# Dense products beside column-tiled runs turned into column tiles, in a fused attention and SwiGLU block on Trainium2

## The chip, the core and the metric

The kernel runs on one core of one Trainium2 chip. A core has TensorE (PE in the profile, PEld for its weight loads), VectorE (DVE), ScalarE (ACT), GpSimd (POOL) and SyncE (SP, which here issues every DMA). The metric is the device time of one execution in microseconds, as the median of several runs; lower is better. Each instruction belongs to one engine's queue and runs there in the order in which it was written; engines wait for one another through semaphores.

## What is computed

A pre-LayerNorm transformer block on 2048 tokens of width 1024, in bf16. Its attention is split into 4 segments of 512 tokens, with 32 heads of 32 elements. Within a segment it is ordinary softmax attention; in addition a memory M (32x32 per head) and its normaliser z are carried from segment to segment, read by the queries and mixed in by a gate. A SwiGLU feed-forward layer of width 3584 follows. Cut to the core:

```python
q, k, v = heads(ln(x) @ wq), heads(ln(x) @ wk), heads(ln(x) @ wv)
for s in range(4):
    p = softmax(qs @ ks.T * scale + mask)
    a_dot = p @ vs
    a_mem = (phi(qs) @ M) / (phi(qs) @ z + 1e-6)
    outs.append(g * a_mem + (1 - g) * a_dot)
    M, z = M + phi(ks).T @ vs, z + sum(phi(ks))
h = x + concat(outs) @ wo
out = h + (silu(ln(h) @ w1) * (ln(h) @ w3)) @ w2
```

## The kernel before

**Dense products.** Projections, the product with wo and the feed-forward layer are written by `mms` (line 707 holds its `matmul`): groups of eight (28 for w2) products of 128x128 weights with 128x512 moving data that add up in one bank of PSUM. A group is cut into steps of four products, and each step is one operation of the order list. Eight banks exist; scores take banks 0 to 3, dense groups mostly 5, 6 and 7.

**Scores** (line 1079). A head has 32 elements, so four heads are computed at once: TensorE is split into four row tiles of 32x128, one for each head, and each writes its own bank of 0 to 3. ACT then takes the exp of all four banks in one instruction (line 1093), and POOL masks the diagonal. There are ten such operations for each of the eight half segments (4 segments, 2 halves of 16 heads).

**Column-tiled runs** (`finish`, lines 1165, 1172 and 1000). When the ten exps of a half segment are done, numerators (exp times v), denominators and the memory's products phi(k) times v are computed with TensorE split into four column tiles of 128x32. Numerators of head j go to bank j, denominators to bank 4, the memory's products to bank 7.

**Retrieval** (line 1296): 16 tiles of 32x32 compute phi(q) times M, in banks 0 to 3.

So TensorE runs in four modes: full, row, column and 32x32. Each operation has its mode written in `mode`. The kernel puts dense steps between scores, so that TensorE has work while ACT takes the exp.

**What sets the order.** No scheduler runs. The table `ORDER` at the top lists, for each engine, the numbers of the operations in the order in which they are issued; `BANKS` gives the bank of each group, and `HOLD` a few transfers that are kept back. `schedule` reads them, and `emit` writes the instructions with their semaphores.

**The start.** `constants` clears a buffer and runs 12 products on zeros (`warm`) before any data is there. The first four tiles of x are normalised (`first_tile`: statistics on DVE and ACT, the power -1/2 on POOL, line 880, the scaling on DVE, line 884), transposed on TensorE (line 719) and copied out of PSUM (lines 730 and 731). `first_half` issues their loads and those of the first weights, in pieces, and the first projections run on 128 tokens at a time.

Of the kernel before, what the change touches and what calls it, by code (L numbers as in the profile page):

```python
# [9 lines left out]
F32 = DT.float32  # L10
# [242 lines left out]
class Graph:  # L253
# [150 lines left out]
    def schedule(self):  # L404

        ops = self.ops
        order = {}
# [1083 lines left out]
```

## Time and profile before

| | |
|---|---|
| time of the runs | 884.87 us median of 3 (884.76 to 886.7) |
| the profiled execution, first to last instruction | 882.6 us |
| median of the runs less that span | 2.2 us (launch and end; the views give no time of their own for the profiled execution beyond its span) |
| TensorE products (PE) | 877.7 us busy (99%), 5821 instructions |
| weight loads (PEld) | 398.1 us (45%) |
| DVE, ACT, POOL | 50%, 34%, 18% |
| granted TensorE clock, mean | 1.000 |
| DMA | 105.75 MB, mean 120 GB/s |

A row of the timeline gives start, length, engine, line, operation, `out<-in`, the tile of TensorE as rows*columns, the shape, and how many instructions were merged. Products overlap in the pipeline, so the time that one costs is the distance from its start to the next one's start, not its length. In lists of groups the last column is the idle time of the engine just before them, with what ended it.

### The profile page before, as it was taken

The page shows a single profiled execution, that of the slowest core. Times are in us where ns is not written, and L with a number is a line of the kernel's source. Part 1 is how long each engine was busy: PE and PEld are TensorE (multiplying, and loading weights), DVE is VectorE, ACT ScalarE, POOL GpSimd, SP SyncE. Part 2 cuts the span into 40 slices and gives each one's busy share as a digit, 9 for nine tenths or more (in the row PEclk, how much of TensorE's full clock was granted, in tenths as well). Part 3 has the DMA queues.
Part 4 walks back from the last instruction along what each step waited for, and adds up shares of the span by engine and source line. Part 5 has one row for each costly group of instructions (what it writes and reads, how often), then busy time and mean ns, then how long its engine had stood idle before and what let it go on. Part 6 is the DMA issues. An engine that isn't in the chain of part 4 may idle for free.

```text
span 882.6 us, 13741 instructions
## 1 busy us (share of the span) xinstructions
PE 877.7 (99%) x5821; PEld 398.1 (45%) x5821; DVE 439.5 (50%) x735; ACT 301.7 (34%) x345; POOL 162.9 (18%) x226
## 2 busy tenths in 40 slices
PE   8999999999999999999999999999999999999998
PEld 5443444444444444444444444444444444444445
DVE  5787878876666777745354301322243344231011
ACT  5878675768656655511111000111011111110000
POOL 1534344335242444303000000000000000000000
PEclk9999999999999999999999999999999999999999
DMA  7989938555962627395483411211322322201011
GB/s 227 214 185 215 251 85 225 144 144 161 233 158 82 168 68 172 93 283 160 113 242 95 113 36 30 78 54 54 96 76 62 96 72 61 89 7 48 19 42 42
DMA packets 148956, 105.75 MB, mean 120 GB/s; under 512 B 46368, under 2 KB 134688, under 8 KB 147872
## 3 DMA queue, kind: packets, MB, share of 16 engines
q1 hardware_dynamic: 148896, 104.89, 45.8%
q8 instruction: 46, 0.75, 0.4%
q14 instruction: 14, 0.11, 0.0%
HBM read 84.94 MB, written 9.44 MB: 107 GB/s over the span
## 4 chain that ended last, share of the span: by engine, by line
PE 99%; DMA 1%; SPq 0%; issue 0%; DVE 0%; DVEq 0%
PE ps L707 92%; PE ps L1079 3%; PE ps L1172 3%; DMA wp<-in_A_wk_dram 1%; PE ps L1000 0%; PE ps L1296 0%; SPq L388 0%; PE ps L1165 0%; PE ps L719 0%; DVE ob L1401 0%; DVEq L524 0%
## 5 line engine op out<-in xcount | busy, mean ns | idle before, releaser
L707 PE MATMUL ps<-hnT,w1b 128*128 128x512 bf16 x896 | 216.2, 379 | 0.0
L707 PE MATMUL ps<-hnT,w3b 128*128 128x512 bf16 x896 | 213.9, 379 | 0.0
L707 PE MATMUL ps<-w2b,hm 128*128 128x512 bf16 (+2 forms) x952 | 199.2, 366 | 0.0
L1369 ACT ACTIVATE sg<-ps 128x512 bf16<-128x512 f32 x112 | 66.8, 597 | 385.5 <-PE ps L707 384.3
L1372 DVE SCALAR_TENSOR_TENSOR t<-sg,ps 128x512 bf16<-128x512 bf16 x112 | 76.6, 685 | 190.1 <-ACT sg L1369 189.8
L1093 ACT ACTIVATE et<-ps 128x2048 bf16<-128x2048 f32 x80 | 150.1, 1876 | 47.7 <-PE ps L1079 45.8
L707 PEld LDWEIGHTS ps<-w2b,hm 128*128 128x128 bf16 x952 | 90.9, 98 | 103.2 <-issue 0.3
L707 PEld LDWEIGHTS ps<-hnT,w1b 128*128 128x128 bf16 x896 | 86.3, 98 | 105.6 <-issue 5.6
L707 PEld LDWEIGHTS ps<-hnT,w3b 128*128 128x128 bf16 x896 | 86.4, 98 | 105.3 <-issue 3.1
L1102 POOL TENSOR_SCALAR_AFFINE_SELECT et<-et 128x512 bf16<-128x512 bf16 (+1 forms) x96 | 83.1, 877 | 112.5 <-ACT et L1093 112.5
L1377 DVE SCALAR_TENSOR_TENSOR hm<-t,ps 128x512 bf16<-128x512 bf16 x112 | 76.2, 684 | 42.5 <-PE ps L707 40.6
L1401 DVE TENSOR_TENSOR ob<-hr,ps 128x512 bf16<-128x512 bf16 (+2 forms) x34 | 21.9, 654 | 122.4 <-PE ps L707 122.3
L707 PE MATMUL ps<-xnT,wp 128*128 128x512 bf16 (+1 forms) x352 | 60.9, 321 | 1.1 <-DMA wp<-in_A_wk_dram 1.1
L707 PE MATMUL ps<-wo,oT 128*128 128x512 bf16 x256 | 61.1, 380 | 0.0
L707 PE MATMUL ps<-hnT,wp 128*128 128x512 bf16 x256 | 59.7, 380 | 0.0
L1118 DVE TENSOR_TENSOR sum<-sum,et 128x512 bf16<-128x512 bf16 (+1 forms) x64 | 40.5, 640 | 6.1 <-POOL et L1102 3.8
L707 PEld LDWEIGHTS ps<-xnT,wp 128*128 128x128 bf16 x352 | 27.9, 98 | 27.3 <-issue 3.5
L707 PEld LDWEIGHTS ps<-wo,oT 128*128 128x128 bf16 x256 | 23.8, 98 | 29.7 <-issue 3.0
L707 PEld LDWEIGHTS ps<-hnT,wp 128*128 128x128 bf16 x256 | 23.6, 98 | 29.7 <-issue 3.7
L1079 PE MATMUL ps<-qT,kT 32*128 32x128 bf16 (+3 forms) x512 | 31.7, 301 | 0.0
L1341 DVE TENSOR_TENSOR h<-h,ps 128x512 bf16<-128x512 bf16 x32 | 21.6, 679 | 20.2 <-PE ps L707 19.8
L707 PE MATMUL ps<-wp,hnT 128*128 128x512 bf16 x128 | 30.4, 380 | 0.0
(101 smaller groups left out, 568.2 us busy)
## 6 DMA issues: line engine op xcount, KB each, us to landing
w1b<-in_B_w_dram SPq DMA_DIRECT2D x28, 512.0 KB, 4.1
w3b<-in_B_w_dram SPq DMA_DIRECT2D x28, 512.0 KB, 4.4
wp<-in_A_wv_dram SPq DMA_DIRECT2D x8, 1024.0 KB, 5.9
wp<-in_A_wq_dram SPq DMA_DIRECT2D x7, 1024.0 KB, 6.2
wp<-in_A_wk_dram SPq DMA_DIRECT2D x7, 1024.0 KB, 7.6
w2b<-in_B_w_dram SPq DMA_DIRECT2D x7, 1024.0 KB, 5.8
h<-in_A_x_dram SPq DMA_DIRECT2D x16, 256.0 KB, 3.0
h_scr<-h SPq DMA_DIRECT2D x16, 256.0 KB, 3.3
```

The costliest lines, as they stand in the source:

```text
L707: return [e.matmul(p[0](gr), p[1], p[2], start=p[3], stop=p[4]) for p in part]
L1079: ins.append(e.matmul(self.bank(gr, j, 512 - 128 * kc, off), k[r, g0 + g, 128 * kc:128 * kc + 128], q[r, g0 + g, 128 * kc:512], start=True ...
L1093: return [e.activation(et[:, :, :], src, AF.Exp, scale=self.scale)]
L1102: self.pool_op(lambda e, v=v, pat=pat: e.affine_select(v, v, pattern=pat, compare_op=ALU.is_ge, fill=0.0, base=0, channel_multiplier=-1), ...
L1118: lambda e, gr: [e.tensor_tensor(o, a, b, op=ALU.add) for o, a, b in sums],
L1172: ins.append(e.matmul(self.ps[32 * i:32 * i + 32, b * 512 + c0:b * 512 + c0 + n], lhsT(i, kc, j), rhs(i, j), start=kc == 0 and j == first, ...
L1341: self.g.op("dve", dve_ns(512), lambda e, gr, hs=hs: [e.tensor_tensor(hs, hs, self.bank(gr), op=ALU.add)], reads=[hs], writes=[hs], cls=1, ...
L1369: self.g.op("act", act_ns(512), lambda e, gr, sg=sg: [e.activation(sg, self.bank(gr), AF.Tanh, scale=0.5)], writes=[sg], cls=0, group=gg)
L1372: e.scalar_tensor_tensor(t1, sg, 1.0, self.bank(gr), op0=ALU.add, op1=ALU.mult)], reads=[sg], writes=[t1], cls=0,
L1377: e.scalar_tensor_tensor(dst, t1, 0.5, self.bank(gr), op0=ALU.mult, op1=ALU.mult)], reads=[t1], writes=[dst], cls=0,
L1401: self.g.op("dve", dve_ns(n), lambda e, gr, hs=hs, ob=ob, n=n: [e.tensor_tensor(ob, hs, self.bank(gr, 0, n), op=ALU.add)], reads=[hs], wri ...
```

## The change

1. `mms` may now write a dense step in two ways: as before, or as column tiles: each 128x128 product becomes four, which take 32 columns of the weights each, read the same moving data and write 32 partitions each of the same bank. A new function `shape` chooses: it walks the order of PE, and a stretch of dense steps becomes column tiles when one neighbour of the stretch is in column mode and neither neighbour is in full mode (the transposes and the program's ends count as full).
2. `ORDER`, `BANKS` and `HOLD` are made anew. In PE's order, scores stand directly beside the runs that are in column mode.
3. The first load of key weights (8 chunks of 128 rows, 256 columns) becomes two loads of 4 chunks each, and so every number in the tables from there on grows by one.
4. The warm-up has 10 products in place of 12, and POOL sets the small constant `mhalf` ahead of the identity.

```diff
 ORDER = {
     "pe": (
-        "1 30 33-34 86 84-85 87 45 80 48 82-83 81 88 90 94 91 56 89 59 92 95 93 102 100 98 70 99 "
+        "1 34-35 31 83 81-82 84 46 85 49 87 91 89 92 90 57 88 86 93 60 94 97 101 95-96 98 103 71 "
...
+        self.shape(order["pe"])
...
+    def shape(self, pe):
+
+        i = 0
+        while i < len(pe):
+            j = i
+            while j < len(pe) and pe[j].free:
+                j += 1
+            sides = {pe[k].mode if 0 <= k < len(pe) else "full" for k in (i - 1, j)}
+            if "col" in sides and "full" not in sides:
+                for o in pe[i:j]:
+                    o.mode = "col"
+            i = j + 1
...
-            last.mode = "full"
+            last.mode, last.free = "full", True
+
+            def emit(e, gr, part=part, op=last):
+                if op.mode == "full":
+                    return [e.matmul(p[0](gr), p[1], p[2], start=p[3], stop=True,
+                                     skip_group_check=True) for p in part]
+                return [e.matmul(p[0](gr)[32 * j:32 * j + 32, :], p[1][:, 32 * j:32 * j + 32], p[2],
+                                 start=p[3], stop=True, tile_position=(0, 32 * j),
+                                 skip_group_check=True) for p in part for j in range(4)]
...
-        self.warm(12)
+        self.warm(10)
+        mh = self.mhalf[:, :]
+        P(lambda e: e.memset(mh, -0.5), 1, [], [mh], 0)
...
-                 (wk[:, :, 0:256], sk[:, :, 0:256]), (wq[:, :, 256:512], sq[:, :, 256:512]),
+                 (wk[:, 0:4, 0:256], sk[:, 0:4, 0:256]), (wk[:, 4:8, 0:256], sk[:, 4:8, 0:256]),
+                 (wq[:, :, 256:512], sq[:, :, 256:512]),
```

In the changed file the dense products stand at lines 734 (full) and 736 (column tiles), the scores at 1108, the column-tiled runs at 1194, 1201 and 1029, the retrieval at 1325, the transposes at 747 and the DMAs at 395.

**How the orders moved: TensorE, into the first column-tiled run.** Rows of PE's queue in the first half segment, before the change: xnT is the normalised and transposed x, wp the projection weights (wp_114 those of v), qT and kT the queries and keys, et an exp.

```order
L1079 MATMUL ps<-qT_77,kT_78 128x128 x4
L1079 MATMUL ps<-qT_77,kT_78 128x384 x4
L707 MATMUL ps<-xnT,wp_71 128x512 x4
L707 MATMUL ps<-wp_114,xnT 128x512 x4
L707 MATMUL ps<-xnT,wp_71 128x512 x4
L707 MATMUL ps<-wp_114,xnT 128x512 x8
L1172 MATMUL ps<-et_88,v_79 32x512
```

The same place in the changed kernel:

```order
L1108 MATMUL ps<-qT_77,kT_78 128x128 x4
L1108 MATMUL ps<-qT_77,kT_78 128x384 x4
L736 MATMUL ps<-xnT,wp_71 32x512 x64
L736 MATMUL ps<-wp_114,xnT 32x512 x16
L1201 MATMUL ps<-et_88,v_79 32x512
```

Twenty dense products stand between the last scores and the first numerators in both; now they are 80 column tiles, and TensorE goes from row tiles to column tiles without the full mode between.

**TensorE, out of the same run.** Before, in the last rows of the run and behind it (hnT holds the normalised and transposed x of the next segment here):

```order
L1172 MATMUL ps<-et_97,v_79 32x128
L707 MATMUL ps<-wp_114,xnT 128x512 x12
L1079 MATMUL ps<-qT_77,kT_78 128x512 x4
L707 MATMUL ps<-hnT_68,wp_70 128x512 x12
L1079 MATMUL ps<-qT_77,kT_78 128x128 x4
L1079 MATMUL ps<-qT_77,kT_78 128x384 x4
```

And in the changed kernel (sum_105 and ones are the run's denominators, pkn the keys of the memory's products):

```order
L1201 MATMUL ps<-sum_105,ones_50 32x256 x2
L736 MATMUL ps<-wp_114,xnT 32x512 x16
L1108 MATMUL ps<-qT_77,kT_78 128x512 x4
L736 MATMUL ps<-wp_114,xnT 32x512 x16
L1029 MATMUL ps<-v_79,pkn 32x33 x16
L736 MATMUL ps<-hnT_68,wp_70 32x512 x32
L1108 MATMUL ps<-qT_77,kT_78 128x128 x4
L1108 MATMUL ps<-qT_77,kT_78 128x384 x4
```

The next half segment's first scores moved into the run, ahead of its last memory products, and the dense products on both sides of them are column tiles.

**SP, the first loads.** Before:

```order
L388 DMA xs_72<-in_A_x_dram 128x512 x2
L388 DMA xs_73<-in_A_x_dram 128x1024
L388 DMA xs_74<-in_A_x_dram 128x1024
L388 DMA xs_75<-in_A_x_dram 128x1024
L388 DMA wp_71<-in_A_wk_dram 128x8x256
L388 DMA wp_70<-in_A_wq_dram 128x4x256 x2
```

In the changed kernel:

```order
L395 DMA xs_72<-in_A_x_dram 128x512 x2
L395 DMA xs_73<-in_A_x_dram 128x1024
L395 DMA xs_74<-in_A_x_dram 128x1024
L395 DMA wp_70<-in_A_wq_dram 128x4x256 x2
L395 DMA wp_71<-in_A_wk_dram 128x4x256
L395 DMA xs_75<-in_A_x_dram 128x1024
L395 DMA wp_71<-in_A_wk_dram 128x4x256
```

Both halves of the first query weights and the first half of the key weights now stand ahead of the fourth tile of x, and the first projections use the query weights, where those of before used the key weights.

More of the change, by code (lines that the diff above doesn't have):

```diff
@@ L31 @@
     "pe": (
[60 rows of a table removed]
-    "act": (
[17 rows of a table removed]
-    "dve": (
[38 rows of a table removed]
-    "pool": (
[27 rows of a table removed]
[60 rows of a table added]
+    ),
+    "act": (
[17 rows of a table added]
+    ),
+    "dve": (
[39 rows of a table added]
+    ),
+    "pool": (
[10 rows of a table added]
+    ),
[16 rows of a table added]
+    ),
 }
 BANKS = (
-    "3013010101567456755566775656676655656756755567567577657576000000000001247300000000000124"
-    "7375567655567677566557565665675765000000000001247300000000000012473557676655775676676577"
-    "6560000076755675000000012473000000000000124730000000000001243000000000000124305665575675"
-    "6576575675675675675677565107316576556756756756756401646765645112176123477516566067147512"
-    "6240464765741742104645620164175406601654602543517712717317717447771275715174547354727176"
-    "7543567254614167726564776675635274511652665361546457121514574023412547765765674557405765")
+    "3123010210567475565775576657765756776756755656567667757576000000000001247300000000000124"
+    "7367567665577757565765555676656655000000000001247300000000000012473765757565577656767675"
+    "7650000056676565000000012473000000000000124730000000000001243000000000000124303445475774"
+    "7546574564567654675465767216336576574556746754546043632745375473136332650417403553712432"
+    "3620647165471732107615230134071246601254602543031736714317717447711727215114347346122517"
+    "6475436245714713762524176675637254711652632331546547524314374023123517014164573102754317"
+)
 HOLD = (
[3 rows of a table removed]
[3 rows of a table added]
 )
@@ L198 @@
                  "ready", "start", "end", "pos", "signal", "tok", "group", "first", "last",
-                 "mode", "bytes", "kind", "snap", "gate", "port", "patience", "offered", "unit", "hush")
+                 "mode", "bytes", "kind", "snap", "free", "gate", "port", "patience", "offered", "unit", "hush")
     def __init__(self, engs, cost, emit, cls, seq):
@@ L213, in __init__ @@
         self.mode = None
+        self.free = False
         self.bytes = 0
@@ L600, in plan @@
         self.beta = buf("beta", [128, 32], BF16)
+        self.mhalf = buf("mhalf", [128, 1], F32)
         self.gcol = buf("gcol", [128, 8], F32)
         self.ocol = buf("ocol", [128, 8], F32)
-        self.mhalf = buf("mhalf", [128, 1], F32)
         self.Mbf = buf("Mbf", [128, 8, 32], BF16)
@@ L704, in mms @@
             cost = sum(mm_ns(p[5]) for p in part)
-            def emit(e, gr, part=part):
-                return [e.matmul(p[0](gr), p[1], p[2], start=p[3], stop=p[4]) for p in part]
             used = part if eager or i else items
-            last = self.g.op("pe", cost, emit, reads=[p[1] for p in used] + [p[2] for p in used],
+            last = self.g.op("pe", cost, None, reads=[p[1] for p in used] + [p[2] for p in used],
                              cls=cls, group=group)
-            last.mode = "full"
+            last.mode, last.free = "full", True
[6 more added lines that the diff above has]
+                                 skip_group_check=True) for p in part for j in range(4)]
+            last.emit = emit
         return last
@@ L776, in constants @@
                                     base=0, channel_multiplier=1), 128, [i], [i], 0)
-        mh = self.mhalf[:, :]
-        P(lambda e: e.memset(mh, -0.5), 1, [], [mh], 0)
         o = self.ones32[:, :, :]
```

286 rows, old and new, of tables (HOLD, ORDER) are left out of this document.

## The prediction

> **What bounds the kernel now.** I read the page first: the engines' shares, the chain that ended last, and the costly groups of products (the last column of a group is the idle time of its engine just before it).
>
> ```profile
> PE 877.7 (99%) x5821; PEld 398.1 (45%) x5821; DVE 439.5 (50%) x735; ACT 301.7 (34%) x345; POOL 162.9 (18%) x226
> PE 99%; DMA 1%; SPq 0%; issue 0%; DVE 0%; DVEq 0%
> L707 PE MATMUL ps<-hnT,w1b 128*128 128x512 bf16 x896 | 216.2, 379 | 0.0
> L707 PE MATMUL ps<-xnT,wp 128*128 128x512 bf16 (+1 forms) x352 | 60.9, 321 | 1.1 <-DMA wp<-in_A_wk_dram 1.1
> L1079 PE MATMUL ps<-qT,kT 32*128 32x128 bf16 (+3 forms) x512 | 31.7, 301 | 0.0
> q8 instruction: 46, 0.75, 0.4%
> ```
>
> TensorE is the bound, and it is not only busy: no large group has idle time ahead of it but the first projections, 1.1 us behind a load of key weights. So nothing on DVE, ACT or POOL pays unless it makes TensorE wait, and the change can win in two ways alone: make TensorE's own stream shorter, or start it earlier. Since "busy" counts pipelined products as one long bar, I next read the timeline of PE for the spacing of starts. These are rows from a stretch of plain dense products (396 to 404 us) and from one with score products (255 to 262 us); the columns are start and length in us.
>
> ```profile
> 397.01 2.75 PE L707 MATMUL ps<-hnT,w1b 128*128 128x512 bf16 x12
> 399.60 4.48 PE L707 MATMUL ps<-hnT,w3b 128*128 128x512 bf16 x20
> ...
> 257.30 2.76 PE L707 MATMUL ps<-hnT,w3b 128*128 128x512 bf16 x12
> 260.00 0.39 PE L1079 MATMUL ps<-qT,kT 32*128 32x512 bf16 x4
> 260.32 1.90 PE L707 MATMUL ps<-hnT,w1b 128*128 128x512 bf16 x8
> ```
>
> Twelve dense products take 399.60 - 397.01 = 2.59 us, 0.216 each. With one group of scores (four row tiles at once, 512 columns, again worth 0.216) the same twelve take 260.32 - 257.30 = 3.02 us. Thirteen times 0.216 is 2.81, so 0.21 us goes into the two changes of tiling, 0.105 each. Next the column-tiled run of the last half segment (362 to 372 us), and the start of a fully tiled group.
>
> ```profile
> 364.56 2.75 PE L707 MATMUL ps<-hnT,w3b 128*128 128x512 bf16 x12
> 367.24 2.36 PE L1172 MATMUL ps<-et,v 128*32 128x512 bf16 x64
> 369.43 0.39 PE L1165 MATMUL ps<-pq,zsel 128*32 128x512 bf16 x4
> 369.64 0.23 PE L1172 MATMUL ps<-et,ones 128*32 128x128 bf16 x4
> ...
> 370.42 0.28 PE L1172 MATMUL ps<-sum,ones 128*32 128x256 bf16 x4
> 370.63 1.68 PE L707 MATMUL ps<-hnT,w1b 128*128 128x512 bf16 x7
> ...
> 394.81 1.03 PE L707 MATMUL ps<-hnT,w3b 128*128 128x512 bf16 x4
> 395.77 0.43 PE L1296 MATMUL ps<-pq,Mbf 32*32 32x512 bf16 x16
> ```
>
> Into the columns: 367.24 - 364.56 = 2.68 less 2.59 is 0.09. Out of them: 370.63 - 370.42 = 0.21 less half of 0.216 (256 columns) is 0.10. Into the 32x32 tiles, where rows and columns are split at once: 0.96 less 4 x 0.216 is 0.10. So every kind of change shown costs 0.09 to 0.106, whatever the two modes; I take 0.103. And a group of four column tiles at 512 columns takes 369.64 - 369.43 = 0.21, as long as one dense product.
>
> **The change part by part.** *Dense products as column tiles.* By the order of both kernels, 416 of the 3,665 dense 512-column products become four column tiles each (1,664 instructions at L736). At 0.216 for four, that costs nothing. What the trace doesn't show is four column tiles that read the same moving operand: in L1172 and L1165 each reads its own. Bounds: 0 (as L1165), up to 416 x 0.01 = 4 us if each group cost the 0.01 that rounding and start-up leave open. I take 0: L1165 is the nearest, with four strips of one tensor.
>
> *Changes of tiling.* The order of before has 190 changes of mode: 80 into and 80 out of row tiles, 9 and 9 for column tiles, 6 and 6 for 32x32 tiles. The order of the changed kernel has 172: 71 full to row, 70 row to full, 10 row to column, 9 column to row, 5 full to tile, 6 tile to full, 1 column to tile. A column run used to be entered from and left to dense products; now the dense products between it and the nearest scores are themselves column tiles, and nine scores moved there. Eighteen fewer changes at 0.103 are -1.85 us. All of it lies on the chain, since PE has no idle time there. Twenty changes are of pairs that the trace doesn't show (row or tile directly against column). Bounds: as cheap as 0.09 (0.3 us better) up to two ordinary changes each (20 x 0.103 = 2.06 us worse); the 32x32 row, which changes both splits for 0.10, is the nearest, so I take 0.103. The Trainium skill's page "TensorEngine Tiling (Array Packing)", Key Properties, says that a change of tiling mode drains TensorE, and its page "TensorE: Matmul & The Clock Gate", Step-by-step, puts the drain at about 128 cycles, which as an estimate is 0.053 us at 2.4 GHz and would make this sum 18 x 0.053 = 0.96 us. The rows show twice that per change, so the trace decides.
>
> *The start.* These are the timeline's rows of the first 14 us on which it hangs.
>
> ```profile
> 1.24 5.30 PE L707 MATMUL ps<-oT 128*128 128x512 bf16 x12 [1.24 <-DVE oT L772]
> 3.12 0.43 SPq L388 DMA_DIRECT2D wp<-in_A_wk_dram  x1
> 4.83 0.56 POOL L880 TENSOR_TENSOR rstd<-lnve,mhalf 128x1 f32<-128x1 f32 x1 [3.39 <-DVE lnve L879]
> 6.07 0.72 DVE L884 TENSOR_SCALAR xs<-xs,lnmv,rstd 128x512 bf16<-128x512 bf16 x2
> 7.17 1.08 ACT L730 ACTIVATE xnT<-ps 128x512 bf16<-128x512 bf16 x2
> 8.35 0.73 DVE L884 TENSOR_SCALAR xs<-xs,lnmv,rstd 128x512 bf16<-128x512 bf16 x2
> 8.66 1.07 PE L707 MATMUL ps<-xnT,wp 128*128 128x128 bf16 x16 [1.08 <-DMA wp<-in_A_wk_dram]
> ...
> 13.03 0.73 DVE L884 TENSOR_SCALAR xs<-xs,lnmv,rstd 128x512 bf16<-128x512 bf16 x2
> ```
>
> The first projection starts at 8.66, when the key weights (512 KB, issued sixth, at 3.12) have landed. Now half of the query weights (256 KB) stands fifth on SP, in the place of the last tile of x, and the first projections read it; 0.5 MB less has to land before it is there, a third of the 1.5 MB that had landed by 8.66. What comes last then is the copy of the transposed tile: ACT's two copies start at 7.17, behind statistics that haven't moved, and the first is over by about 7.8. So the first projection may start at 7.8, 0.85 us sooner. But the second tile is still normalised only at 8.35 and the last at about 13.0, because the chain through DVE, POOL and ACT is as long as before (and the last x lands later, behind three weight loads). PE, which had no wait after 8.66, will now catch up with it and wait between transposes. I keep half: -0.4 us; bounds 0 and -0.85. The warm-up of 12 products becomes 10: they run at 0.43 us each, the half clock, and end 0.85 us sooner, before the first transposes in either case; if the clock rose one microsecond later for it, that would cost 0.5 us. Three more POOL memsets now stand ahead of the first rstd at 4.83; POOL idled 3.39 us there, which covers them.
>
> *Order lists.* All engines have new orders. Scores still stand behind at least 12 dense products, as before (the 3.02 us period above), so each exp has the room it had:
>
> ```profile
> L1093 ACT ACTIVATE et<-ps 128x2048 bf16<-128x2048 f32 x80 | 150.1, 1876 | 47.7 <-PE ps L1079 45.8
> ```
>
> An exp takes 1.88 us of that 3.02. Nine scores now stand close behind numerators, whose banks 0 to 3 have to be copied out first. Counted in products by the order, the shortest way from the last numerator in a bank to the next score is 1.89 us, against 1.92 before, and there PE didn't wait. I put new waits at +0.1 us, bounds 0 and 3.
>
> *More instructions.* PE gets 1,246 more products with their weight loads; 11,642 PE instructions came in 46 fetches, so some ten fetches are added. One hold-up in a column run may be such a fetch:
>
> ```profile
> 178.59 0.18 PE L1000 MATMUL ps<-v,pkn 128*32 128x33 bf16 x1
> 179.05 0.27 PE L1000 MATMUL ps<-v,pkn 128*32 128x33 bf16 x15 [0.28 <-issue]
> ```
>
> It took 0.46 us once in 46 fetches; ten more are worth +0.1 us, bounds 0 and 1.
>
> Sum: -1.85 - 0.4 + 0.1 + 0.1 = -2.05 us on the profiled span of 882.6 us, so 880.6. The median of the runs is 884.87, 2.2 us above that span for what lies around it; the same 2.05 off gives 882.8 us.
>
> **The rivals.** (a) *The start comes whole*: PE keeps all 0.85 us, and no wait is added. For it: before, PE ran from 8.66 without a wait, so there was slack in the chain. Against it: the normalised tiles come no sooner. -1.85 - 0.85 = -2.7: 882.2.
> (b) *A direct change from row to column tiles costs as much as two*: +2.06 on the sum, 884.9. Against it: the 32x32 row.
> (c) *Waits take the place of the changes*: a score next to a column run waits for a copy that stands behind an exp of 1.88 us on ACT. One such at each of two of the eight runs less the slack gives about +2: 884.8. Against it: the distances are as before.
> (d) *Slower: a dense product as four column tiles costs more than 0.216.* Its place is the 416 groups at L736, above all the 104 in a row ahead of the last 32x32 group; its mechanism is four small weight loads and four reads of one moving operand in the time of one. It eats the gain from 5 ns per group on, and makes the kernel slower by over 0.3% from 11 ns on: at 12 ns, 416 x 0.012 = 5.0, so 887.8. Against it: the sixteen products of 33 columns below, each with its own 32-column load, take 0.10 us in all, 6 ns per load, so loads hide easily under 0.216.
>
> ```profile
> 177.63 0.27 PE L1000 MATMUL ps<-v,pkn 128*32 128x33 bf16 x16
> 177.73 0.23 PE L1172 MATMUL ps<-et,ones 128*32 128x128 bf16 x4
> ```
>
> The Trainium skill's page "TensorEngine Tiling (Array Packing)", Restrictions and Gotchas, speaks for (d): column tiling shuts off the fast weight load. The 6 ns per load say that this doesn't show at 32 columns.
>
> That the change doesn't do what it says can be ruled out: the order has the 172 changes.
>
> **How the numbers follow.** Forecast 0.52, (a) 0.22, (b) 0.08, (c) 0.11, (d) 0.07. What a measurement here can tell from no change is about 0.3%, 2.65 us: under 882.2 is faster, over 887.5 slower. Case (a) lies on that line, and the forecast's better end (cheaper direct changes, more of the start) passes it: faster 0.32. Slower is case (d) and the worst of (c): 0.08. The rest, 0.60, is the same. The range reaches down to (a) with direct changes at 0.09 and some products over, 881.4, and up past (b) and (c) to 885.6; (d) and little else is left out.
>
> **What would show it.** Right: in the timeline, four L736 tiles every 0.216 us; a 512-column score group to the next L736 group in about 0.32; the first projection near 7.8 us with short waits of PE for DVE and ACT up to 14 us; a span near 880.6. Wrong: L736 groups at 0.22 or more, direct changes at 0.2, or PE's waits by the view of waits holding scores or dense products behind copies after 20 us.

## The result, and the profile after

| | before | after |
|---|---|---|
| median of six runs each | 885.38 us (883.84 to 886.7) | 894.07 us (892.7 to 897.1) |
| ratio | 1 | 1.0098, 95% interval 1.0081 to 1.0115 |
| span of the profiled execution | 882.6 us | 892.3 us |
| changes of tiling mode in PE's order | 190 | 172 |

The changed kernel is 1% slower. I had forecast 882.8 us, with a range of 881.4 to 885.6. The page of the changed kernel has the engines' shares, the shares of the chain that ended last, and the queue that brings instructions:

```profile
PE 877.9 (98%) x7067; PEld 401.4 (45%) x7067; DVE 460.2 (52%) x764; ACT 294.2 (33%) x335; POOL 140.9 (16%) x207
PE 91%; DMA 5%; DVE 3%; issue 0%; SPq 0%; DVEq 0%
q8 instruction: 56, 0.92, 0.4%
```

The ten more fetches are there as forecast (46 to 56), and PE is busy for 877.9 us, as long as before (877.7). But the chain of what ended last, 99% PE before, is now 5% DMA and 3% DVE. PE waits, and the view of PE's waits (engine and tile, what ended the wait; us in all, times, longest) says for what:

```profile
PE ps L1201 <- DVE near L1147: 2.8, 1, 2.8
PE ps L734 <- DMA w3b<-in_B_w_dram: 1.7, 2, 1.5
PE ps L1108 <- DVE Nsb L1255: 1.0, 1, 1.0
PE ps L1108 <- DVE R L1338: 0.8, 3, 0.3
PE ps L734 <- DMA wo<-in_A_wo_dram: 0.5, 1, 0.5
PE ps L1201 <- DMA pkn<-pk: 0.5, 1, 0.5
PE ps L734 <- DVE hm L1406: 0.5, 1, 0.5
PE ps L734 <- DMA out_dram<-ob: 0.3, 1, 0.3
```

None of these was there before; they make 8.1 us. (The waits of the start are left out; Nsb is the copy of the numerators out of PSUM, which frees their banks, R holds reciprocals of the denominators, hm the feed-forward layer's products.) The largest can be followed back. These are rows of the changed kernel's timeline, of PE, then DVE, then SP:

```profile
95.79 0.72 PE L1201 MATMUL ps<-et,v 128*32 128x512 bf16 x16
99.31 0.24 PE L1201 MATMUL ps<-et,ones 128*32 128x128 bf16 x4 [2.80 <-DVE near L1147]
```

```profile
91.87 0.54 DVE L897 TENSOR_SCALAR xs<-xs,lnmv,rstd 128x1024 bf16<-128x1024 bf16 x1
96.88 0.69 DVE L862 BATCH_NORM_STATS2 lnst<-xs 128x6 f32<-128x512 bf16 x1 [4.46 <-DMA xs<-in_A_x_dram]
97.48 0.68 DVE L759 CAST kT<-ps 128x512 bf16<-128x512 f32 x1
98.41 0.75 DVE L1147 TENSOR_TENSOR near<-et,et 128x512 bf16<-128x512 bf16 x2
```

```profile
84.43 1.40 SPq L402 DMA_TRANSPOSE hnT<-xs  x1
85.87 5.21 SPq L402 DMA_TRANSPOSE pkn<-pk  x1
92.17 0.36 SPq L395 DMA_DIRECT2D xs<-in_A_x_dram  x1
```

DVE's list has a LayerNorm statistic of a coming segment ahead of `near`, a sum that the denominators need. The statistic stands still for 4.46 us until its x has landed. That x was issued at 92.17, because SP's list has the transpose that empties the same buffer only at 84.43, and by the view of transfers that transpose took 7.7 us to land. So PE, which was done with its numerators at 96.3 (by the spacing of starts), waits for an addition that has nothing to do with that x. In the kernel before, the same load left at 85.7 and the statistic stood behind `near`:

```profile
85.69 1.40 SPq L388 DMA_DIRECT2D xs<-in_A_x_dram  x1
...
91.36 0.75 DVE L1118 TENSOR_TENSOR near<-et,et 128x512 bf16<-128x512 bf16 x2
92.63 0.68 DVE L834 BATCH_NORM_STATS2 lnst<-xs 128x6 f32<-128x512 bf16 x1
```

The 1.0 us for Nsb, at 58.71, has the same cause: three statistics stand ahead of that copy on DVE, and the first stands still for 2.64 us until its x lands at 56.0. The other waits, 4.3 us in all, were not followed back in this trace. The wait for `near` has a second price, which the windows show (start and end, length, busy time of each engine, then granted clock, share of DMA, GB/s):

```profile
95.00:100.00 5.00, 2.20 (x100) 1.40 (x92) 3.09 (x7) 0.69 (x1) 0.00 (x0) 1.00 1.15 196
100.30:103.70 3.40, 3.40 (x70) 1.62 (x58) 3.15 (x7) 2.10 (x3) 0.00 (x0) 0.50 1.09 345
```

The clock falls to half for 3.4 us after PE has come back; half of it, 1.7 us, is lost. So the span's 9.7 us are 8.1 of waits and 1.7 of clock, less 1.85 for the changes of mode that went, and 1.75 more. Most of these 1.75 are the same waits again: the view counts idle time from the end of a product's row, and the rows overlap. From start to start, less the products' own price, the eleven waits cost 9.5 us (the one for `near` 99.31 - 96.33 = 2.98), which leaves 0.3 us open. The start gives nothing (below).

The form of the products itself does what was forecast. In PE's timeline, 32 column-tile instructions (8 products) take 386.00 - 384.28 = 1.72 us, 0.215 a product. A score group straight into column tiles (58.71 to 59.04, 0.33 less 0.216) and out of them into scores (60.02 to 61.85, 1.83 less 1.73) costs about 0.11 and 0.10:

```profile
58.71 0.40 PE L1108 MATMUL ps<-qT,kT 32*128 32x512 bf16 x4 [1.01 <-DVE Nsb L1255]
59.04 1.05 PE L736 MATMUL ps<-wp,xnT 128*32 128x512 bf16 x16
...
60.02 1.90 PE L736 MATMUL ps<-hnT,wp 128*32 128x512 bf16 x32
61.85 0.40 PE L1108 MATMUL ps<-qT,kT 32*128 32x128 bf16 x8
...
384.28 1.90 PE L736 MATMUL ps<-hnT,w3b 128*32 128x512 bf16 x32
386.00 2.76 PE L736 MATMUL ps<-hnT,w1b 128*32 128x512 bf16 x48
```

### The profile page after: what moved, and what is told of

It reads as the page before. It is cut to its first block, busy times and chain, and to the rows that moved or that the text cites. A ratio compares the mean times of both kernels' runs of the same rounds, so it can differ in the third digit from the quotient of the medians.

```text
span 892.3 us, 16193 instructions
## 1 busy us (share of the span) xinstructions
PE 877.9 (98%) x7067; PEld 401.4 (45%) x7067; DVE 460.2 (52%) x764; ACT 294.2 (33%) x335; POOL 140.9 (16%) x207
## 4 chain that ended last, share of the span: by engine, by line
PE 91%; DMA 5%; DVE 3%; issue 0%; SPq 0%; DVEq 0%
PE ps L734 76%; PE ps L736 9%; PE ps L1108 3%; PE ps L1201 2%; DMA w3b<-in_B_w_dram 1%; DMA xs<-in_A_x_dram 1%; DVE R L1338 1%; DMA hnT<-xs 1%; DMA wo<-in_A_wo_dram 1%; DMA wp<-in_A_wq_dram 1%; DMA out_dram<-ob 0%; DVE sum L1147 0%; SPq L395 0%; DVE lnst L862 0%; PE ps L1325 0%
## 5 line engine op out<-in xcount | busy, mean ns | idle before, releaser
L734 PE MATMUL ps<-hnT,w1b 128*128 128x512 bf16 x808 | 194.5, 379 | 0.5 <-DVE hm L1406 0.5
L734 PE MATMUL ps<-hnT,w3b 128*128 128x512 bf16 x788 | 189.4, 379 | 1.7 <-DMA w3b<-in_B_w_dram 1.7
L734 PEld LDWEIGHTS ps<-hnT,w1b 128*128 128x128 bf16 x808 | 77.6, 98 | 96.5 <-issue 4.0
L734 PEld LDWEIGHTS ps<-hnT,w3b 128*128 128x128 bf16 x788 | 75.5, 98 | 95.3 <-issue 4.4
L734 PE MATMUL ps<-xnT,wp 128*128 128x512 bf16 (+1 forms) x316 | 53.2, 315 | 1.6 <-DMA wp<-in_A_wq_dram 0.9
L734 PE MATMUL ps<-wo,oT 128*128 128x512 bf16 x220 | 53.0, 380 | 0.5 <-DMA wo<-in_A_wo_dram 0.5
L734 PE MATMUL ps<-hnT,wp 128*128 128x512 bf16 x168 | 39.0, 380 | 0.0
L734 PEld LDWEIGHTS ps<-xnT,wp 128*128 128x128 bf16 x316 | 24.5, 98 | 24.1 <-issue 3.3
L734 PEld LDWEIGHTS ps<-wo,oT 128*128 128x128 bf16 x220 | 20.6, 98 | 26.7 <-issue 2.7
L1147 DVE TENSOR_TENSOR sum<-et,et 128x1024 bf16<-128x1024 bf16 x32 | 24.6, 773 | 5.9 <-ACT et L1122 5.8
```

The source lines that it names most:

```text
L734: return [e.matmul(p[0](gr), p[1], p[2], start=p[3], stop=True, skip_group_check=True) for p in part]
L1147: lambda e, gr: [e.tensor_tensor(o, a, b, op=ALU.add) for o, a, b in sums],
```

## The experiments

Thirteen runs. The first theory after the traces was: the form is sound, the order lists cost the time, and they do so by statistics that stand on DVE ahead of what PE needs. The first rival: the column form itself costs it. (Rivals of the experiments have capital letters, those of the prediction small ones. Each cut of code shows the edit against the kernel that its paragraph names.)

**The form alone.** The kernel before with its own lists and loads, and only the form changed:

```diff
+    def shape(self, pe):
...
+            if "col" in sides and "full" not in sides:
+                for o in pe[i:j]:
+                    o.mode = "col"
...
+                return [e.matmul(p[0](gr)[32 * j:32 * j + 32, :], p[1][:, 32 * j:32 * j + 32], p[2],
+                                 start=p[3], stop=True, tile_position=(0, 32 * j),
+                                 skip_group_check=True) for p in part for j in range(4)]
```

> The kernel before with its own order lists and loads, and only the form changed: 87 runs of dense work (348 products) that stand next to column-tiled runs become four column tiles each. That leaves 172 mode changes of 190, as many as in the changed kernel. Theory (the form is sound, the order lists cost the time): 18 changes less at 0.103 us = 1.85 us less than before, span near 880.8, time near 883.5, and no wait on PE over 0.5 us. Rival A (the column form itself costs what was lost): no gain, at or above before's time, and over 885.4 by up to 9 us.

Measured: 894.45 us, 1.0112 of before (1.0099 to 1.0125), span 893.5. The first theory missed by eleven us, and the time is where rival A had it. The view of PE's waits has three rows that are missing in both kernels, where "issue" had 0.3 us:

```profile
PE ps L730 <- issue: 4.4, 2, 2.6
PE ps L728 <- issue: 1.5, 1, 1.5
PE ps L1194 <- issue: 1.2, 1, 1.2
```

"issue" means that PE waited for no engine and no transfer that the profile knows. The longest, in the middle of a run of column tiles, and the clock after it:

```profile
233.40 1.46 PE L730 MATMUL ps<-wo,oT 128*32 128x512 bf16 x21
237.50 1.47 PE L730 MATMUL ps<-wo,oT 128*32 128x512 bf16 x11 [2.65 <-issue]
```

```profile
237.30:240.70 3.40, 3.20 (x18) 0.84 (x19) 0.00 (x0) 1.13 (x1) 0.22 (x2) 0.50 0.73 91
```

A step is four products, so 16 instructions here, and PE stops five into its second: a place where the program waits for nothing. I then counted PE's instructions in the trace (weight loads, products, waits) up to each of the four standstills, and looked up the 16 KB packets of the instruction queue, some 256 instructions each (11,845 of PE's, 203 waits and the like among them, came in 46 in the kernel before). The first column has the start of the last product ahead of the standstill, and the count can be off by one:

| PE stands from | instruction | remainder by 256 | instruction packet | PE goes on |
|---|---|---|---|---|
| 58.5 us | 1217 | 193 | 57.05 to 58.67 | 60.0 |
| 100.1 | 2241 | 193 | 98.66 to 100.90 | 102.2 |
| 143.1 | 3264 | 192 | 142.33 to 143.36 | 145.0 |
| 234.5 | 5313 | 193 | 234.87 to 235.91 | 237.5 |

PE has used up its instructions; each time it goes on 1.3 to 1.6 us after the packet. In the quiet last third of the kernel such a packet starts 204 to 296 instructions before the standstill's place that it serves. Dense full products use 300 instructions in 32 us, column tiles in 8, the short denominators in less, while packets had landed mostly 2 to 6 us after the point 297 instructions ahead where other transfers were busy. The rest of this run's loss is the half clock (1.7 us) and its start: the first scores came 3.6 us later than in the kernel before, behind a key load that landed late and half clock until 15.4 us. Of four later runs with the same start, three had the first scores at 17.4 to 17.7 us, as before, and one at 19.6, so that part isn't the form's alone; why these two had it stays open.

**The lists alone.** The changed kernel without the call of `shape`, so that every dense product is full.

```diff
-        self.shape(order["pe"])
```

> The changed kernel with its order lists and loads, and every dense product in its full form: 224 mode changes, 34 more than before. Theory (the order lists cost the time): before's time plus 34 x 0.103 = 3.5 us plus the same waits of about 10 us, so 896 to 899 us, above the changed kernel, with the waits of 3.0 us near 96 us and 1.7 us near 406 us still there. Rival A (the loss belongs to the column form): before's time plus the 3.5 us alone, about 889, and below the changed kernel.

Measured: 896.8 us, 1.0133 of before (1.0118 to 1.0147). The time came as the theory had it, the waits not all: `near` took 0.4 us, not 3, and in its place a feed-forward product waited for a copy of the keys from 255.8 to 258.0 us, with the half clock behind it.

```profile
PE ps L733 <- DVE kT L758: 2.2, 1, 2.2
PE ps L733 <- DMA w3b<-in_B_w_dram: 1.4, 1, 1.4
```

So the lists lose without the form too, by waits that move about as soon as PE's pace differs by a few us. And there was no standstill at remainder 193. The form alone costs 10.0 us, the lists alone 12.4, both 8.7: the two losses don't add up. With the new lists the packets keep up with the column tiles (no such standstill in the changed kernel), and the form takes 52 of the 224 changes of mode away again, 5.4 us at 0.103 each.

**DVE's list mended**, and then PE's list as well.

```diff
-        "403 238 237 214 423 420 179 421 419 435 426 436 239 427 231 428-429 439 292 213 431 279 "
+        "403 423 238 237 214 420 179 421 419 435 426 436 239 427 231 428-429 439 292 213 431 279 "
...
-        "481 454 486 340 321 491 218 270 337 492 506 656 331 657 503 660 311 79 501-502 78 507 "
+        "481 454 486 340 321 491 218 337 492 506 270 656 331 657 503 660 311 79 501-502 78 507 "
```

> The changed kernel with two places of DVE's list altered: the statistics of xs stand behind the Nsb copy near 55 us, and behind the two near additions and the sum near 92 us, in place of ahead of them. Theory (DVE's operations that PE needs stand behind statistics that wait for a late load): the waits of 3.0 us at 96 us and 1.0 us at 57 us go, and with the first of them the half clock from 100.3 to 103.7 us that cost about 1.6 us: 5.5 us less than the changed kernel, near 888.5, granted clock full from 5 us on. Rival B (the loads set the pace wherever the statistics stand, so the wait only moves to the next operation that PE needs): within 1 us of the changed kernel, a wait of 2 us or more within 15 us of the old place.

```diff
-        "1716 1634 1717-1719 1711 1636 1730 1338 1709 1712 1710 1731 1748 1486 1732 1723 1733 "
+        "1716 1634 1717-1719 1711 1636 1730 1338 1709 1712 1710 1731 1486 1732 1748 1723 1733 "
```

> As the run before it, and on PE the step whose weights load late near 406 us stands 8 dense products later. Theory: 1.5 us below the kernel with only DVE's list altered, near 887, no wait for that load over 0.3 us. Rival B (the load lands later too, since its buffer is freed later): within 0.4 us of the kernel with only DVE's list altered.

Measured: 896.07 us (1.0136 of before, 1.0112 to 1.0161) and 893.43 (1.0103, 1.0088 to 1.0119). Moving the statistics gained nothing: the time is 2 us above the changed kernel's, with runs from 893.8 to 901.9, and new waits came where rival B had them. The w3b wait went; the medians differ by 2.6 us where 1.5 was expected, but the two intervals overlap, so its price isn't settled by this. Where the DVE waits had gone, the second kernel's timeline of DVE and PE shows:

```profile
94.57 0.75 DVE L1253 TENSOR_SCALAR Nsb<-ps,ocol 128x512 f32<-128x512 f32 x1
97.91 0.69 DVE L860 BATCH_NORM_STATS2 lnst<-xs 128x6 f32<-128x512 bf16 x1 [2.59 <-issue]
100.05 0.75 DVE L1253 TENSOR_SCALAR Nsb<-ps,ocol 128x512 f32<-128x512 f32 x1
101.04 0.69 DVE L757 CAST v<-ps 128x512 bf16<-128x512 f32 x1
```

```profile
100.94 0.40 PE L1106 MATMUL ps<-qT,kT 32*128 32x512 bf16 x4 [1.77 <-DVE Nsb L1253]
107.50 0.81 PE L732 MATMUL ps<-hnT,wp 128*128 128x512 bf16 x3 [2.17 <-DVE v L757]
```

`near` is in time now, but the same statistic holds up the next things that PE needs, the second Nsb copy and the copies of v. (Its row names no releaser; its x left SP at 93.25, and 4.7 us, as that load took in the changed kernel, lead to 97.9.)

**The form where instructions can keep up.** The code theory had to be tried against the rival that the column form is dear wherever it stands. From the run of the form alone, `shape` now turns 8 of its 17 stretches:

```diff
+            if j > i and "col" in sides and "full" not in sides:
+                if nth in (6, 7, 8, 9, 12, 14, 15, 16):
+                    for o in pe[i:j]:
+                        o.mode = "col"
+                nth += 1
```

> The run with the form alone lost 10 us although it kept the order lists before: PE stood still at four places (1.4, 1.9, 1.7 and 2.8 us), each time at an instruction whose number, counted on PE, leaves 193 when divided by 256, and a 16 KB instruction load was under way or just landed. New theory (code): four column tiles are eight instructions where a full product is two, and where such products follow short column work PE uses up its instructions before the next 256 land. Here only 8 of the 17 runs of dense work get the form (204 of 348 products, the 116 near 380 us among them), chosen so that by step prices PE needs 5.2 us or more for the last 297 instructions before each such boundary; 181 mode changes of 190. Code: no standstill at a boundary over 0.5 us, 9 x 0.103 = 0.9 us below before. Rival A (the column form itself is dear, wherever it stands): 204/348 of 10 us, about 6 us above before.

Measured: 883.54 us, 0.9987 of before (0.9975 to 0.9999), span 881.1; no standstill over 0.5 us at a boundary. 1.2 us below before where 0.9 was forecast, with 204 products as column tiles; the interval only just excludes no gain. Rival A's 6 us are excluded by the interval.

**As many instructions without column tiles.** Against the run of the form alone, the same products are cut in four along the moving operand and stay in the full form.

```diff
-                return [e.matmul(p[0](gr)[32 * j:32 * j + 32, :], p[1][:, 32 * j:32 * j + 32], p[2],
-                                 start=p[3], stop=True, tile_position=(0, 32 * j),
+                return [e.matmul(p[0](gr)[:, 128 * j:128 * j + 128], p[1],
+                                 p[2][:, 128 * j:128 * j + 128], start=p[3], stop=True,
                                  skip_group_check=True) for p in part for j in range(4)]
```

> The kernel before with its own order lists; the same 348 products as in the run of the form alone are split in four, but along their moving columns (128 each) and in the full form: as many instructions as there, no column tile, 190 mode changes. By the price of a full 128-column product (55.7 ns) the split itself costs 348 x 7 ns = 2.4 us at most. Code: 7 to 12 us above before, with standstills of 1 us and more at instructions that leave 193 when divided by 256, near 58, 100, 143 and 235 us. Rival A (the column form is what costs): 0 to 2.4 us above before, without them.

Measured: 898.28 us, 1.0153 of before (1.0134 to 1.0172), 13.6 us above it, a little over the forecast 7 to 12 (the first scores came 1.9 us late here too). PE stood at 57.0, 98.6, 141.8 and 235.1 us (for 0.5, 1.8, 2.4 and 2.8 us; the first was to be 1 us and more), the same four places, the longest again after 21 of 32:

```profile
233.98 1.34 PE L730 MATMUL ps<-wo,oT 128*128 128x128 bf16 x21
238.13 1.36 PE L730 MATMUL ps<-wo,oT 128*128 128x128 bf16 x11 [2.80 <-issue]
```

These are full-form products. With the run before it, this shows that the number of instructions costs the time, and that the column form does not.

**SP's list**, to bring the loads earlier, once on the changed kernel and once on the kernel with DVE's and PE's lists mended.

```diff
-        "187 276 212 361 236 289 315 441 328 476 227 302 482 243 437 466 268 470 515 493 235 577 "
+        "187 236 276 212 361 289 315 441 328 476 227 243 302 482 268 437 466 470 515 493 235 577 "
```

> The changed kernel with SP's list altered at two places: a load of xs goes out ahead of the wq load near 45 us (6 us earlier), and the transpose of xs and the reload of its buffer go ahead of a wv load, a wo load and a pkn transpose near 80 us (about 5 us earlier each). DVE's list is the changed kernel's. Theory (a late load of xs holds up DVE, and DVE the numerators): the waits of 3.0 us at 96 us and 1.0 us at 57 us go, with the half clock after the first: 4 to 5.6 us below the changed kernel. Rival B (the transfers are the bound there, so an earlier issue only lets others land later): within 1 us of it, waits of 2 us or more on another transfer within 15 us.

> The kernel with DVE's and PE's lists altered, and SP's as well: theory: the waits of 1.8 and 2.2 us for Nsb and v near 99 and 105 us and that of 1.5 us near 58 us, which DVE's new order had left, go too: 5 us below the kernel without SP's alteration, near 888. Rival B: within 1 us of it.

Measured: 898.95 us (1.0167 of before) and 901.1 (1.0181): worse by 5 and by 8 us than without the edit. The wait for `near` did go. But the x load that was moved ahead still had to wait on SP, until 50.6 us, and held up what stands behind it: the 1 MB of query weights left at 50.9 in place of 45.5, and a transpose of the keys behind them landed at 60.4 in place of 55.4, late for the denominators at 54 us. The clock fell to half for 6.8 us. In the first of the two:

```profile
PE ps L1201 <- DMA pkn<-pk: 6.3, 1, 6.3
PE ps L1029 <- issue: 1.8, 1, 1.8
```

The second row is PE at a boundary of its instructions again, near 102 us (1.8 us): with other moments, the new lists no longer keep clear of it.

**DVE's statistics moved on further.** All statistics that wait now stand behind the copies that PE needs next.

```diff
-        "403 423 238 237 214 420 179 421 419 435 426 436 239 427 231 428-429 439 292 213 431 279 "
+        "403 423 420 179 421 419 238 237 214 435 426 436 239 427 231 428-429 439 292 213 431 279 "
...
-        "481 454 486 340 321 491 218 337 492 506 270 656 331 657 503 660 311 79 501-502 78 507 "
-        "500 269 314 661 305 509 508 589 510 77 511 271 580 736 602 512 679 596 261 684 682 253 "
+        "481 454 486 340 321 491 218 337 492 506 656 331 657 503 660 311 79 501-502 78 507 "
+        "500 314 305 661 509 508 270 269 589 510 77 511 271 580 736 602 512 679 596 261 684 682 253 "
```

> The kernel with DVE's and PE's lists altered (SP's as in the changed kernel), and all statistics of xs that wait for the late loads moved on behind the copies that PE needs next: near 57 us behind the v cast, near 92 to 106 us behind Nsb, both v casts and two oT products. Theory (DVE's queue behind late loads is what costs in the changed order): the waits for Nsb (1.8 us at 99), v (2.2 us at 105) and v (1.5 us at 58) go: 4 to 5.5 us below the kernel with the first alteration, near 888.5. Rival B (these waits come back behind the next operation, because DVE has no room left between 90 and 110 us): within 1 us of that kernel.

Measured: 893.69 us (1.009 of before, 1.0071 to 1.0109), as with the smaller edit. The waits for Nsb and for v are down to 0.2 and 0.5 us, and still nothing is won, for PE now waits at 102 us for something that DVE has no part in:

```profile
101.87 1.23 SPq L400 DMA_TRANSPOSE hnT<-xs  x1
```

```profile
106.14 3.32 PE L732 MATMUL ps<-hnT,wp 128*128 128x512 bf16 x8 [3.69 <-DMA hnT<-xs]
```

Rival B was right in the time and wrong in the reason: DVE's copies came in time.

**The cause put into a kernel that doesn't have it.** The kernel with 204 column products, one statistic put ahead of `near` (as in the changed kernel), and then its load made late as well.

```diff
-        "680 474 375 463 681 464 333 485 480 490-491 339 253 500 505 252 499 254 501 506 268 310 "
+        "680 474 375 463 681 464 333 485 480 490 268 491 339 253 500 505 252 499 254 501 506 310 "
```

> The fast kernel with the form on 204 products, and the one statistic of xs that stands behind near, kT and four more on DVE put ahead of near (at about 89 us); its load leaves SP at about 86 us as before and lands by about 92. Theory (what costs is a statistic whose load is late, not its place alone): near comes at most 1 us later, and PE uses it 1.6 us after it is there: no wait on PE for near over 0.3 us, time within 1 us of the kernel without the alteration. Rival D (any work put ahead of near costs PE its length): 0.7 us and up, with a wait for near.

```diff
-        "219 211 227 275 235 288 436 440 454 226 459 314 251 469 465 327 475 242 218 234 267 301 "
-        "576 589 481 243 492 486 514 259 657 529 661 615 274 521 340 545 602 641 737 250 536 528 "
+        "219 211 227 275 235 288 436 440 454 226 459 314 251 469 465 327 475 242 218 234 301 "
+        "576 589 267 481 243 492 486 514 259 657 529 661 615 274 521 340 545 602 641 737 250 536 528 "
```

> As the run before it, and the load of that statistic leaves SP behind three weight loads, at about 93.6 us in place of 85.7, as it does in the changed kernel. Theory: it lands near 98.3, near follows near 99.5, and PE stands about 6 us at the numerators from 93.5 us on, after which the clock falls to half for a while (3.4 us, about 1.6 us lost): 6 to 9 us above the kernel without the alteration. Rival D: the same small loss as with the place alone, under 2 us.

Measured: 883.15 us for the place alone (0.9977 of before, 0.9964 to 0.999; no wait for `near`), and 895.85 with the late load (1.0117, 1.0093 to 1.0142). 12.7 us, more than the 6 to 9 expected, because the load, behind 2 MB of weights, landed not at 98.3 but at 102.2:

```profile
102.24 0.69 DVE L858 BATCH_NORM_STATS2 lnst<-xs 128x6 f32<-128x512 bf16 x1 [11.55 <-DMA xs<-in_A_x_dram]
```

```profile
PE ps L1196 <- DVE near L1142: 10.8, 1, 10.8
```

The clock was at half from 96.6 to 106.9 us, and PE worked in the last 2.8 us of it, which lost 1.4 more. So this mechanism is shown: a statistic's place on DVE costs nothing as long as its load is there, and the load's delay in full when it isn't.

**What makes the transposed x late** in the kernel with DVE clear. Its transpose ahead of the reload that waits in front of it, then ahead of the wq load too.

```diff
-        "260 219 590 658 487 455 662 460 252 530 616 522 244 341 546 603 537 642 275 267 529 738 "
+        "219 260 590 658 487 455 662 460 252 530 616 522 244 341 546 603 537 642 275 267 529 738 "
```

> The run before it with DVE's statistics moved on (890.2 us of span), and on SP the last transpose of the normalized xs (hnT<-xs at 101.9 us there) put ahead of the reload of xs, which stood in front of it and waited 4.6 us for the transpose before that. Theory (in the changed order DVE is clear now, and SP's list makes this transpose late): it goes out near 97 us, PE's wait of 3.7 us at 102 us goes, and with it the half clock of 3.4 us after it (1.6 us lost): 4 to 5.3 us below the run before, span near 885.5, time near 889. Rival B (the transfers are the bound): the transpose lands no earlier, within 1 us of the run before.

```diff
-        "187 276 212 361 236 289 315 441 328 476 227 302 482 243 437 466 268 470 515 493 235 577 "
-        "260 219 590 658 487 455 662 460 252 530 616 522 244 341 546 603 537 642 275 267 529 738 "
+        "187 276 212 361 236 289 315 441 328 476 227 302 482 243 437 466 268 470 515 493 235 219 "
+        "577 260 590 658 487 455 662 460 252 530 616 522 244 341 546 603 537 642 275 267 529 738 "
```

> As the run with DVE's statistics moved on, and on SP the last hnT transpose goes ahead of the 1 MB wq load as well as of the reload of xs. In the run before it stood right behind that load: it went out at 96.8 us in place of 101.9, and landed at 105.1 all the same, 8.3 us later. Theory (SP's list makes it late, by what it puts ahead of it in the transfers' queues): issued near 96.2 us it lands by about 101.5, PE's wait of 2.7 to 3.7 us at 102 us goes and with it the half clock after it (1.6 us): 4 to 5.3 us below the run with DVE's statistics moved on, near 889. Rival B (what is short there is the transfers' time in all, so the time comes back in the next load that PE needs, the wq load first): within 1 us of it, a wait of 2 us or more for wq or another load before 120 us.

Measured: 893.61 us (1.011 of before, 1.0092 to 1.0127) and 893.99 (1.0103, 1.0081 to 1.0125): rival B both times. SP and PE of the first, then of the second:

```profile
96.18 0.58 SPq L393 DMA_DIRECT2D wp<-in_A_wq_dram  x1
96.81 4.53 SPq L400 DMA_TRANSPOSE hnT<-xs  x1
...
105.45 3.45 PE L732 MATMUL ps<-hnT,wp 128*128 128x512 bf16 x8 [2.74 <-DVE oT L1303]
```

```profile
94.16 4.88 SPq L400 DMA_TRANSPOSE hnT<-xs  x2
99.09 0.58 SPq L393 DMA_DIRECT2D wp<-in_A_wq_dram  x1
...
105.92 3.57 PE L732 MATMUL ps<-hnT,wp 128*128 128x512 bf16 x8 [3.47 <-DVE lnst L860]
```

By the view of transfers the transpose of the first landed 8.3 us after its issue, at 105.1, and the wq load of the second 6.5 us after, at 105.6; PE goes on 0.35 us behind each, as it did behind the late transpose of the kernel with DVE clear (landed 105.79, PE at 106.14), so the transfers are taken as the cause, although PE's rows name DVE. Whichever goes first, the other is late, with both let out from 94 us on; the kernel before had its transposes out by 85.7 and the wq load at 92.6. To put SP's whole old list into the changed kernel wasn't tried. So it stays open how much of the changed kernel's loss a better list for SP alone would give back.

## Why the prediction was wrong

- **The form at no cost, and the changes of tiling at -1.85 us.** Right. A product as four column tiles takes 0.215 us, and direct changes between row and column tiles cost what ordinary ones do. Nine changes less brought 1.2 us in the run with 204 column products, within its interval of the 0.9 forecast. Rivals (b) and (d) fall.
- **The start at -0.4 us.** It came out at about 0. The first projection starts at 7.42 us (7.8 forecast), behind ACT's copy as forecast, but PE then waits 0.9 us for the query weights, and while the first scores come 0.83 us sooner, four dense products (0.86 us) now stand behind them that stood ahead.
- **The order lists at +0.1 us, bounds 0 and 3. This is the step that failed.** It measured 8.1 us of waits by the view (9.5 from start to start) and 1.7 of half clock. I had compared one distance, from a numerator to the next score, counted in PE's own products. What decides is on the other engines' lists: what stands on DVE ahead of each copy or sum that PE needs, which load that waits for, and when SP's list lets the load out. The orders could be read before the run; the landing times only roughly (the load moved on purpose was expected at 98.3 and landed at 102.2). Rival (c) named the kind (waits in place of the changes) with the wrong place, ACT's exp, and a fifth of the size.
- **More instructions at +0.1 us, bounds 0 and 1.** Right for the changed kernel, which has 0.3 us of "issue", and wrong as a reason. I priced fetches by their number. The hold-up of 0.46 us that I quoted as "one in 46" was PE at such a boundary, with nothing to spare; under the old lists the same form costs 7.1 us there. The number held by luck: nothing in the sum asked whether the new lists leave room.
- **What would make it wrong** was named rightly: the view of PE's waits has scores and denominators behind copies and sums after 20 us.

## What to carry to other kernels

When a hand-made order is replaced, look in each engine's list for an operation that waits for a load and stands ahead of one that the bound engine needs, and price it with the load's issue and landing; the bound engine's own list doesn't tell. Before cutting products into smaller instructions, work out how long the bound engine takes for its next 300 instructions and compare it with the time of a fetch under load (mostly 2 to 6 us here). In the run where the form paid, PE had about 5 us or more; the four places with standstills had 2.8 to 4.3, though a few places with 3.4 to 4.7 ran through. The kernel with 204 column products on the old lists (883.54 us, 0.9987 of before) is below both kernels, if by little.

## What the runs showed of the hardware

- PE's instructions come in packets of some 256, and PE can stand still in the middle of a step for one, 0.5 to 2.8 us here, without any semaphore; its instruction's number then leaves 193 by 256 in this program, and the idle time is put down to "issue".
- Half clock came in pieces of 3.41 us or a multiple: 3.41 in the changed kernel after 3.0 us between two starts, 6.83 after 6.6, 10.24 after 11.0 (but 6.83 after 3.9 in the last run). The full clock before it, from 4.71 to 100.28 us in the changed kernel, is 28 such pieces. Past the kernel's first 20 us, it did not come after gaps of 1.9 to 2.55 us, and after 2.6 to 2.8 in two cases of four. The Trainium skill's page "TensorE: Matmul & The Clock Gate", in What's actually happening, has the clock judged by free-running windows of 3.413 us, which agrees with these lengths; its rule under HAM oscillation, that gaps over about 3.4 us are to be avoided, is too lenient here, since gaps of 2.6 to 3.0 us between starts were enough.
- A transpose by DMA right behind a 1 MB load took 8.3 us to land, and 3.9 us when that load was issued 5.6 us ahead of it: with its issue 5 us sooner it landed only 0.7 us sooner, at 105.1. Issued ahead of the load, at 95.4, it landed at 102.6.
